# Linear attention with a mixture of experts on one core: the key sums of the last 24 head pairs, from TensorE's products with ones to a GpSimd reduction and a scatter

## The chip, the cores and the metric

The kernel runs on one core of a Trainium2 chip. The metric is the device time of one execution in microseconds, as the median of several runs. Lower is better.

## The reference, cut to what matters

Eight batches with eight heads each, 576 positions, head dimension 64, 128 features. Heads are taken in pairs: pair p holds two heads, and four pairs make a batch, so there are 32 pairs.

```
phi(x): proj = x @ w_phi; proj -= max|proj|;  [exp(proj), exp(-proj)]     # 256 features
kv  = sum over s of phi(k)[s,f] * v[s,d]        # 256 x 64 a head
z   = sum over s of phi(k)[s,f]                 # 256 a head
out = (phi(q) @ kv) / (phi(q) @ z + 1e-6)       # attention
x = out; four experts: causal softmax attention of x, times wo, weighted by the best two gates
```

The change is about z, the sum of phi(k) over the positions. phi(k) lies with positions on the partitions, so z is a sum over partitions.

## The kernel before, in words

All work is issued in an order that is written out: the strings `ORDER` and `SIDES` say, step by step, which of the kernel's streams (generators) goes on next and whether a copy goes to ScalarE or VectorE. Each engine carries out its instructions in exactly that order (`in_order` pins it), so an instruction that waits holds up all that stands behind it on its engine. The costs in `plan.run` and `plan.transfer` are a planner's bookings, used when the order was searched; they do not reach the chip.

Work for pair p of the 32:

- `stream_k`, `center`, `phi_k`: keys times w_phi on TensorE, centered on VectorE, exponentials on ScalarE. Four tiles of 128 positions for both heads end in `ek`; the last 64 positions of two pairs share one tile `ekt` (`stream_tails`).
- `key_sum` (pairs 4 to 31): the four position tiles are folded into one, [128, 512], called `zs`. ScalarE writes tiles 0 and 1 into zs; a GpSimd DMA adds tiles 2 and 3 on top (L373, zs<-ek); VectorE adds the two halves (L632); a second GpSimd DMA adds the tail (L373, zs<-ekt). What is left is a sum over 128 partitions. The first 4 pairs have no folding: TensorE sums all four tiles with ones.
- `stream_kv`: 32 matmul records of values times phi(k) (L692, tile shape 128x32), then z as products of `zs` with a matrix of ones (L704, four matmuls that show as eight records of 128 columns), all into one bank of PSUM with three parts a block, 384 columns. From pair 6 on (`KVD`), VectorE transposes the 384 columns out of PSUM into `kvt` (L723), four DMAs on the SP queue scatter it to a buffer in DRAM (kvd<-kvt), and one DMA brings it back as weights, kv (kv<-kvd). `kvd` and `kv` have two buffers.
- `stream_n`: denominators (L790, with the z columns of kv as weights) and numerators (L801) from phi(q) and kv. phi(q) needs a maximum over partitions for each head, which GpSimd forms (L763, PARTITION_ALL_REDUCE of 576 columns); VectorE subtracts it (L765).
- `stream_s`, `maxima`, `stream_t`: the experts' projections (L336), scores (L921), masks on GpSimd (L1029), softmax maxima on GpSimd (L1046, PARTITION_ALL_REDUCE of 1152 columns), attention (L1088, L1117) and the output projection (L336).

`in_order` also makes each PARTITION_ALL_REDUCE wait for the last VectorE instruction before it that takes two inputs from SBUF.

Of the kernel before, what the change touches and what calls it, by code (L numbers as in the profile page):

```python
# [53 lines left out]
KVD = 6  # L54
RATE = 2.18
# [26 lines left out]
def change_cost(a, b):  # L82
# [6 lines left out]
    r'2221111110333388AA27AB1EDE3AB68GC77F8FFG0000BC05BBBB2774@EGI@H@FBB@C@@C3;;1605B2;FFFEEF;FAA;77H6AA@B<JEIEC@C@6'  # L89
    r'BAGG830<8;58G;8II4;BHA;@B;E@<<818AB30F8C@B2;25B7CDC8:A7GCD6CE?EF38:C:BBBFGF;;;BBB00BFE1E24@GGF:5B3D?DE@D:@7FIG'  # L90
    r'72J:EBFD;;?IE:D?;6F6CD7CJCC79908I::432EGG?CD?IEIJGHDD@DEE;;:HH7IAIGG50:H7KG@G@IB?DDDDADDD61AFEB@F=:==:=H=IGA?:'
    r'32F9;9IE??99580EHGG6G6FFE<9E9F9F>>:::E@BFCBABCB963B<CDDB7GGFBDD<FFG7HDDE<HHA9<IHHG@85G8HGG:;=LIH?;;;;;;:HIHHCC'
    r'GGGIBFBHEEGFHGFB=@CAB:C>DA>6=6A48802888838501B?8;FFFAFDCCA=>BB@@:G::@999@?BED??HCDD?7HD8888@8CD78838CD@BGCF8:6'
    r'=FGBJDIJIC:IGH<>=5AGGFD:KGGE<CA9D98888@9D07F7CCHGG=?IIF<CG@HEE?@=828D@C<<DB99=985GGFB=D8FF76KED7JJI?EA?D?::D::'
    r'I:D:D:D<46123<HDCDDDC??=8888?88GE<E?<>CCF=D;839LE;F8<JICH8J988H888I:K5HH:DNGG8HM:J6JLGLJJJDA@BGB:MB:LLL:DJLD=B'
    r'HB::::<;AJKDD?GDAA>HHDEDEDA9IFAC66ACEEAA;;<B8CF7I8?=H?D057242:3K>@CC1E@@KBK>LB=<>LAJE@<<AAB>>ACFED<@IF<@E>?ECD'
    r'FG=B>H:I?CFE:HE:;HI<FGGGDG>?AA9989>88@J==8C008==IFKIFHJB<CEA>D<?@E@D8@>E9G@=>99G88>3CFFGFF>BBF77GGHG7J7III@KF8'
    r'5226GHIF99?18848J80?JNNIAJMJL88HHHHKJHHH>>;;;@876JJ>5B>K8L88>H>J7@D:::><NEFDH<IE::::FM>8G3C6HC88BBD2I?D89KICCJ'
    r'BIIBFBFFFE99FGBB?FF8843?E8888:FEF7I7J2HH@BFH:CJI6JJI:IA5@IA>KH@@H::GDB0A=;L>HHIH966;J?F<<MDHHIG:GMJJGGG?MEH:GK'
    r'KGE<<:<I@=GC?DC<CCCC?AMFCC<<:KB9LBJD>I;98883A8H=CB:B9A8EB=@E?F?F??:5ADEHGA<@CAAAFEFE<:HH7HH:HH7IIH08818880:J2J'  # L100
    r'JJC8CCDBCBBBB99F@D?GD@H83D98GGC?@G@H?7@H6F8G88888EHB5IF7ML<=B>>>Q<GH=D@DEDDDBHDID<A???G8<9KK9LLHD?<>;;;N985IG8'
    r'@<GMLOL0NM2884=M0377NGFIDMLJ?66DCDHHI:::C::::JLCKFM?88188FI<FC<KJ9K9LKEL=HC=FCG8888423888B:HFBG7JIDC?:II6IIII7'
    r'II>:5ONONIHEE:MF:::::1<HJJ8AJ>KIACAFBA;;;<IDJKKIHHNIFFADDIF69:==6=885DE?HE?BHC:K8BIBHBHCCGFEGEFFECBBA<JBHBBC<L'
    r'F300<K=<<99L9JL88<LI888883JKH8H:IIK8>BBBAI@7BG7GB:GH6JJL5NJGJHFJ:FJF9Q9R8<98K880=L4>2>881@8LGGGDD6IDDDDAGECG>E'
    r'8>=H=H==EI57N7EOGG>AAAAE@AFC?C999M>G6G882208838@KG>AIIDJJ>DAHIGHCCCGC99==IFF<G@EF::::JJ=I::BEBDC<KB<C?JHHHG?AJ'
    r'8BB8E:8==88F88848D7G67FHH>J><FFE<DDE5II7L=7;PMINIK>EHH@I;:IJ:ND:IJKJ:@3LACCCL6:K:KMKD6@:::L:;JFFG<JDEBEAEH@BGA'
    r'DDAGAFFADAD9E;CFF;GG88:II;F8:F?:LCCID5CC:HGFMHQKP<<<<GJFCH<F<BEBHHHAECNJCCHHK?KBMHBEAKK999PPCHH1N888308<2IA02H'
    r'I8CC8<>?8?8HFF@77D8=JKIIB4D5C6LI<KDKEEE?DJ>H>K<FC3EFB6<BA<<>9>GGG<@BB?DBA98988?888853E0EFE@EE877L><FGFFD<E>H?G'
    r'6F@AE2C998082@889GGH<FG>EE>C;;;FDGE8@EF<<GAD9IIIA9:=::J::LL:J:EE<HBGGGB?18?C77H=HHCCE:JJJ?G>>838C:KJ6J8KJJ:HII'
    r'GA@>F66A@5EFE:GJG@EE>FD::G:H:I::@9?F@?C?CCBBEBEDE??>D4888=1=71777C@<<@7<:::A96AB9A>=ADGFAFE0BC>>>49=62I9KCAMMA'  # L110
# [197 lines left out]
def tile_linear_attn_moe(ctx, tc, qt, kt, v, wts, out):  # L308
# [12 lines left out]
    def has(*k):  # L321
        return lambda: k in done
# [53 lines left out]
    warm = sb("warm", [128, 128], BF16)  # L376
    nc.vector.memset(warm, 1.0)
    col, ge = sb("col", [128, 128]), sb("ge", [128, 5, 4, 4])
# [30 lines left out]
    kvt = sb("kvt", [128, 4, 96])  # L409
# [26 lines left out]
    gw = col  # L436
# [187 lines left out]
    def key_sum(p, ek, ekk):  # L624
# [13 lines left out]
        done.add(('zt', p))  # L638
        done.add(('zs', p))
# [9 lines left out]
    def tail_products(banks, sums, m):  # L649
        ekt, need = ekts[m % 2], [f'et{m % 2}0', f'et{m % 2}1'] + vtk  # L650
        for h in range(2):
            for k in range(2):
                for a, (pk, ps) in enumerate(banks):
                    r = slice(64 * a, 64 * a + 64)
                    g = 64 * k + 32 * (h ^ a)
                    plan.run('PE', 256 / TRATE / 2 + 5, [pk], need, 64, tiling=(64, 32))
                    nc.tensor.matmul(three(ps)[g:g + 32, 0:2], vt_in[r, h, k:64:2], ekt[r, :, h].rearrange("p c (w f) -> p c w f", w=4),  # L657
                                     start=True, stop=False, skip_group_check=True)
# [8 lines left out]
    def three(ps):  # L667
        return ps[:, 0:384].rearrange("p (w c f) -> p c w f", w=4, c=3)

    def stream_kv():  # L670
# [3 lines left out]
        for p in range(NPAIRS):  # L674
# [10 lines left out]
            o = three(ps)  # L685
# [10 lines left out]
            if adds:  # L696
                yield Step('PE', pred=has('zs', p))
            for t in range(1 if adds else 4):
# [21 lines left out]
            else:  # L720

                yield Step('DVE', pred=has('kvs', p - 1) if p else None)
                dve(384, ['kvt'], [kc], 1.13).transpose(kvt.rearrange("p w n -> p (w n)"), ps[:, 0:384])  # L723
                plan.release('c', (kc, ps))

                for x in range(4):
                    yield Step('SP', pred=has('num', p - 2) if p > 1 else None)
                    load(kvd[p % 2].rearrange("w i x n -> i w x n")[:, :, x, :], kvt[32 * x:32 * x + 32], ('kvd', p % 2, x), ['kvt'])
                kd = [('kvd', p % 2, x) for x in range(4)]
                yield Step('SP')  # L730
# [515 lines left out]
```

## Time and profile before

| what | value |
|---|---|
| median of 3 runs | 575.58 us (574.83 to 576.74) |
| profiled execution: its time / its span | 575.26 us / 573.5 us |
| TensorE's granted clock in the profile | 1.00, that is its 2.4 GHz level, in all slices |
| TensorE (PE), VectorE (DVE), ScalarE (ACT), GpSimd (POOL) busy | 99%, 93%, 79%, 50% of the span |
| the chain that ended last, by engine | PE 92%, ACT 3%, all others 1% or less each |

The span is the stretch in which instructions of the program ran; the 1.8 us between it and the time lie around it. The chain follows the last instruction back, at each step to whatever released it. Busy time on PE is a union of modelled spans, so 99% says that matmuls followed on one another without holes, not that the array ran at its peak.

### The profile page before, as it was taken

How to read it: one execution, taken by the hardware profiler on the slowest of the kernel's cores; microseconds unless marked ns; L12 is line 12 of the kernel's file. 1: busy time of each engine (PE TensorE's matmuls, PEld its weight loads, DVE VectorE, ACT ScalarE, POOL GpSimd, SP SyncE). 2: the span in 40 equal slices, each digit the busy share in tenths (PEclk: the TensorE clock that was granted, in tenths of full speed). 3: DMA queues.
4: the chain of work that ended last, by engine and by line, in shares of the span. 5: the costliest groups of instructions: out<-in, count | busy, mean ns of one | idle time of the engine just before them, and what ended most of it. 6: DMA issues, size and time to landing. Idle time of an engine off the chain costs nothing.

```text
span 573.5 us, 19278 instructions
## 1 busy us (share of the span) xinstructions
PE 567.3 (99%) x7709; PEld 446.5 (78%) x7709; DVE 530.8 (93%) x1134; ACT 455.7 (79%) x1117; POOL 286.0 (50%) x223
## 2 busy tenths in 40 slices
PE   8999999999999999999999999999999999999997
PEld 6666697678877788768877878877887788789886
DVE  6998999999999999999999999999899999999983
ACT  5999989888888868988978887878877886756563
POOL 5467473655367255364735566334645457240530
PEclk9999999999999999999999999999999999999999
DMA  4779666563353653665565643567455462011013
GB/s 137 194 185 227 115 137 144 137 140 90 92 142 95 171 144 75 163 147 121 117 171 128 170 114 52 139 152 184 107 124 135 108 145 57 19 54 64 1 43 126
DMA packets 55785, 69.75 MB, mean 122 GB/s; under 512 B 29328, under 2 KB 34064, under 8 KB 55696
## 3 DMA queue, kind: packets, MB, share of 16 engines
q1 hardware_dynamic: 49184, 49.94, 29.8%
q0 software_dynamic: 6272, 18.35, 19.8%
q8 instruction: 61, 1.00, 0.8%
q10 hardware_dynamic: 240, 0.23, 0.1%
q14 instruction: 28, 0.23, 0.1%
HBM read 35.59 MB, written 14.55 MB: 87 GB/s over the span
## 4 chain that ended last, share of the span: by engine, by line
PE 92%; ACT 3%; DVE 1%; DMA 1%; SPq 1%; POOL 1%; issue 1%; DVEq 0%; POOLq 0%
PE ps_c L336 36%; PE ps_c L551 12%; PE ps_c L801 11%; PE ps_c L692 9%; PE ps_c L921 7%; PE ps_c L1117 7%; PE ps_c L790 5%; PE ps_c L1088 2%; PE ps_c L704 2%; PE ps_c L657 1%; SPq L369 1%; ACT ek L347 1%; DMA kvd<-kvt 1%; POOL mx L763 0%; PE ps_c L715 0%
## 5 line engine op out<-in xcount | busy, mean ns | idle before, releaser
L763 POOL PARTITION_ALL_REDUCE mx<-u x64 | 140.0, 2223 | 64.6 <-ACT u L345 33.7
L336 PE MATMUL ps_c<-x,qk 128*128 128x256 f32 (+1 forms) x768 | 106.9, 298 | 0.0
L336 PEld LDWEIGHTS ps_c<-x,qk 128*128 128x128 f32 x768 | 102.6, 189 | 2.7 <-ACT x L345 0.5
L1046 POOL PARTITION_ALL_REDUCE max<-top x16 | 57.6, 3598 | 42.1 <-DVE top L1042 19.8
L347 ACT ACTIVATE ek<-ek 128x1024 f32<-128x1024 f32 x64 | 67.9, 1061 | 8.3 <-DVE ek L619 7.7
L1029 POOL TENSOR_SCALAR_AFFINE_SELECT s<-s 128x256 f32<-128x256 f32 (+1 forms) x80 | 47.4, 636 | 49.1 <-ACT s L345 23.1
L345 ACT COPY s<-ps_c 64x64 f32<-64x64 f32 (+4 forms) x142 | 52.7, 430 | 15.1 <-PE ps_c L921 14.8
L1050 DVE TENSOR_TENSOR s<-s,max 128x1152 f32<-128x1152 f32 (+4 forms) x80 | 64.2, 835 | 0.4 <-POOL max L1046 0.3
L692 PE MATMUL ps_c<-ek,v_in 128*32 128x256 f32 x1024 | 61.5, 380 | 0.9 <-ACT u L345 0.9
L347 ACT ACTIVATE s<-s 128x384 f32<-128x384 f32 (+4 forms) x80 | 57.5, 739 | 2.9 <-DVE s L1050 2.7
L345 ACT COPY u<-ps_c 128x320 f32<-128x320 f32 (+1 forms) x126 | 46.4, 405 | 15.4 <-PE ps_c L551 12.5
L336 PE MATMUL ps_c<-yh,wo 128*128 128x320 f32 (+1 forms) x256 | 52.6, 300 | 0.0
L373 POOL DMA_DIRECT2D zs<-ek x28 | 25.6, 914 | 53.8 <-ACT ek L347 22.5
L692 PEld LDWEIGHTS ps_c<-ek,v_in 128*32 128x32 f32 x1024 | 32.5, 110 | 24.0 <-issue 3.3
L373 POOL DMA_DIRECT2D zs<-ekt x28 | 23.7, 845 | 55.2 <-DVE zs L632 28.8
L765 DVE TENSOR_TENSOR u<-u,mx 128x576 f32<-128x576 f32 x64 | 50.2, 795 | 0.7 <-POOL mx L763 0.7
L336 PE MATMUL ps_c<-vg,x 128*128 128x260 f32 x384 | 48.7, 285 | 0.4 <-ACT s L345 0.4
L336 PEld LDWEIGHTS ps_c<-vg,x 128*128 128x128 f32 x384 | 47.0, 188 | 1.3 <-ACT s L345 0.6
L1117 PE MATMUL ps_c<-s,vs 128*32 128x320 f32 (+4 forms) x896 | 47.2, 357 | 0.0
L616 DVE TENSOR_REDUCE pmax<-ps_c 128x4 f32<-128x512 f32 x64 | 42.4, 676 | 2.8 <-PE ps_c L551 2.6
L347 ACT ACTIVATE mx<-u 128x576 f32<-128x576 f32 x64 | 43.2, 686 | 2.0 <-DVE u L765 1.7
L1117 PEld LDWEIGHTS ps_c<-s,vs 128*32 128x32 f32 x896 | 29.4, 110 | 19.4 <-issue 0.6
(133 smaller groups left out, 1373.0 us busy)
## 6 DMA issues: line engine op xcount, KB each, us to landing
zs<-ek POOLq DMA_DIRECT2D x28, 512.0 KB, 5.2
q_in<-in_qt_dram SPq DMA_DIRECT2D x62, 144.0 KB, 3.2
k_in<-in_kt_dram SPq DMA_DIRECT2D x64, 128.0 KB, 3.3
v_in<-in_v_dram SPq DMA_DIRECT2D x32, 256.0 KB, 3.1
out_dram<-ot SPq DMA_DIRECT2D x28, 288.0 KB, 3.1
kvd<-kvt SPq DMA_DIRECT2D x104, 48.0 KB, 2.2
kv<-kvd SPq DMA_DIRECT2D x26, 192.0 KB, 2.5
zs<-ekt POOLq DMA_DIRECT2D x28, 128.0 KB, 3.4
```

Source lines behind the costliest of these rows:

```text
L336: nc.tensor.matmul(o, a, b, start=start, stop=stop, skip_group_check=True)
L345: nc.scalar.copy(o, i)
L347: nc.scalar.activation(o, i, func, **kw)
L373: nc.gpsimd.dma_start(o, i, accum_op=ALU.add)
L551: nc.tensor.matmul(o, a, b, start=True, stop=True, skip_group_check=True)
L692: nc.tensor.matmul(o[g, 0:2], v_in[:, 4 * h + t, k:64:2], ek[:, t, :, h, :].rearrange("p c (w f) -> p c w f", w=4), start=False, stop=t == ...
L763: nc.gpsimd.partition_all_reduce(M, U, 128, bass_isa.ReduceOp.absmax)
L765: dve(S, [uk], [mk], port=True).tensor_tensor(out=U, in0=U, in1=M, op=ALU.subtract)
L801: nc.tensor.matmul(ps[g:g + 32, 0:n], kvi[:, 2 * k + (h ^ p % 2), 32 * c:32 * c + 32], P_[h][c][:, s0:s1], start=c == 0, stop=c == 1, skip ...
L1046: nc.gpsimd.partition_all_reduce(big.rearrange("p e s -> p (e s)"), top.rearrange("p e s -> p (e s)"), 128, bass_isa.ReduceOp.max)
L1050: dve(2 * (S - 128 * j), [('d', x, j)], [('max', z)], 1.11, True).tensor_tensor(out=block(s_, j, None, rows(j)), in0=block(s_, j, None, ro ...
L1117: nc.tensor.matmul(ps[r:r + 32, q0 - s0:s1 - s0], vs[:, j, 128 * g + 64 * e + k:128 * g + 64 * e + 64:2], ss[x][:, e, o + q0:o + s1], star ...
```

## The change

`ZP = 8`: pairs 0 to 7 stay as they are. For pairs 8 to 31:

1. The products of zs with ones (L704) are gone. PSUM holds two parts, 256 columns, instead of three, and TensorE's kv products no longer wait for zs.
2. A PARTITION_ALL_REDUCE with add on GpSimd sums zs over the partitions into `zr` [128, 512], after the tail's add.
3. One DMA on the SP queue scatters row 0 of zr to kvd, column 64: 512 runs of one 4-byte word, beside the four DMAs of kv.
4. VectorE's transpose out of PSUM takes 256 columns, and the four DMAs carry 64 columns a block in place of 96. The load of kv waits for five transfers, not four.
5. `warm`, `kvt`, `zr` and `col` become parts of one tile, `shared`; kvt and zr overlap where only pairs before 8 use kvt, and the gates' weights get a tile of their own.
6. `ORDER` (3143 steps in place of 3119) and `SIDES` (520 in both) are new throughout.

```diff
+ZP = 8
 ORDER = (
...
-    kvt = sb("kvt", [128, 4, 96])
+    shared = sb("shared", [128, 768])
+    kvt, zr = shared[:, 0:384].rearrange("p (w n) -> p w n", w=4), shared[:, 256:768]
...
         done.add(('zt', p))
+        if p >= ZP:
+            zk = ['zr', 'kvt'] if p == ZP else ['zr']
+            yield Step('POOL', pred=lambda: p != ZP or ('kvs', p - 1) in done)
+            plan.run('POOL', 3235, zk, k, port=2100)
+            nc.gpsimd.partition_all_reduce(zr, o, 128, bass_isa.ReduceOp.add)
+            yield Step('SP', pred=has('kvs', p - 2))
+            plan.transfer(900, 560, [('kvd', p % 2, 'z')], ['zr'], 'SP')
+            nc.sync.dma_start(kvd[p % 2][:, :, :, 64:65].rearrange("w i x n -> n x (w i)"), zr[0:1, :].rearrange("o (x f) -> o x f", x=4))
         done.add(('zs', p))
...
-            o = three(ps)
+            o = three(ps, 3 if p < ZP else 2)
...
-            if adds:
+            if adds and p < ZP:
                 yield Step('PE', pred=has('zs', p))
-            for t in range(1 if adds else 4):
+            for t in range(0 if p >= ZP else 1 if adds else 4):
...
-                dve(384, ['kvt'], [kc], 1.13).transpose(kvt.rearrange("p w n -> p (w n)"), ps[:, 0:384])
+                n = 384 if p < ZP else 256
+                src = shared[:, 0:n]
+                dve(n, ['kvt'], [kc], 1.13).transpose(src, ps[:, 0:n])
...
-                kd = [('kvd', p % 2, x) for x in range(4)]
-                yield Step('SP')
+                kd = [('kvd', p % 2, x) for x in (range(4) if p < ZP else (0, 1, 2, 3, 'z'))]
+                yield Step('SP', pred=has('zs', p) if p >= ZP else None)
                 load(kv[p % 2].rearrange("p x n -> p (x n)"), kvd[p % 2].rearrange("w i x n -> (w i) (x n)"), f'kv{p % 2}', kd)
```

## Rows read from the trace of the kernel before

**Rows 1.** The page's part 1: busy us, share of the span, instructions.
```profile
PE 567.3 (99%) x7709; PEld 446.5 (78%) x7709; DVE 530.8 (93%) x1134; ACT 455.7 (79%) x1117; POOL 286.0 (50%) x223
```

**Rows 2.** All waits of PE: waiter <- who ended it, us, times, longest.
```profile
PE ps_c L336 <- DVE col L380: 1.0, 1, 1.0
PE ps_c L692 <- ACT u L345: 0.9, 1, 0.9
PE ps_c L336 <- ACT s L345: 0.4, 1, 0.4
PE ps_c L801 <- DVE wided L812: 0.2, 1, 0.2
```

**Rows 3.** Busy us of each engine, 95 to 490 us: pairs 8 to 31.
```profile
95.00:490.00 395.00, 394.31 (x5414) 307.18 (x5408) 375.92 (x796) 323.38 (x803) 210.16 (x165) 1.00 0.54 126
```

**Rows 4.** The chain, 95 to 490 us, by line.
```profile
by line: PE ps_c L336 35.5%; PE ps_c L551 11.4%; PE ps_c L801 11.0%; PE ps_c L692 9.9%; PE ps_c L921 7.2%; PE ps_c L1117 6.7%; PE ps_c L790 5.5%; PE ps_c L657 1.7%; PE ps_c L1088 1.5%; PE ps_c L704 1.2%; SPq L369 1.1%; DMA kvd<-kvt 0.8%; is
```

**Rows 5.** PE by line, 95 to 490 us: busy us, mean ns, idle before.
```profile
L704 PE MATMUL ps_c<-zs,ones 128*32 128x128 f32 x192 | 9.8, 273 | 0.0
```

**Rows 6.** PE in order of time at 286 us: start, us, line.
```profile
286.21 0.40 PE L704 MATMUL ps_c<-zs,ones 128*32 128x128 f32 x8
286.54 1.16 PE L551 MATMUL ps_c<-wf,k_in 64*128 64x128 f32 x16
```

**Rows 7.** The chain, 297 to 312 us: start, us, what, count.
```profile
300.93 0.22 PE ps_c L704 x8
...
309.93 0.22 PE ps_c L704 x8
```

**Rows 8.** DVE by line, 95 to 490 us, same columns as rows 5.
```profile
L765 DVE TENSOR_TENSOR u<-u,mx 128x576 f32<-128x576 f32 x46 | 37.2, 815 | 0.3 <-POOL mx L763 0.3
...
L632 DVE TENSOR_TENSOR zs<-zs 128x512 f32<-128x512 f32 x23 | 18.4, 800 | 0.0
...
L723 DVE STREAM_TRANSPOSE kvt<-ps_c 128x384 f32<-128x384 f32 x24 | 13.7, 569 | 2.6 <-PE ps_c L704 1.4 <-DMA kvd<-kvt 1.0
...
L812 DVE STREAM_TRANSPOSE wided<-ps_c 128x288 f32<-128x288 f32 x23 | 10.7, 464 | 0.5 <-PE ps_c L790 0.5
```

**Rows 9.** POOL by line, 95 to 490 us, same columns as rows 5.
```profile
L763 POOL PARTITION_ALL_REDUCE mx<-u x46 | 101.0, 2231 | 42.8 <-ACT u L345 19.8 <-DVE s L1050 10.4 <-ACT x L345 4.9
L1046 POOL PARTITION_ALL_REDUCE max<-top x12 | 43.1, 3590 | 31.0 <-DVE top L1042 17.9 <-DVE u L765 4.8 <-DVE facy L824 4.4
```

**Rows 10.** DMA issues: queue, count, KB each, median us to landing.
```profile
kvd<-kvt SPq DMA_DIRECT2D x104, 48.0 KB, 2.2
kv<-kvd SPq DMA_DIRECT2D x26, 192.0 KB, 2.5
zs<-ekt POOLq DMA_DIRECT2D x28, 128.0 KB, 3.4
```

**Rows 11.** Lines L765 and L632, whole span: ns minimum/median/maximum.
```profile
L765 DVE TENSOR_TENSOR u<-u,mx x64: 692/748/2124, 10.6 to 489.7; 128x576 f32<-128x576 f32 x64
...
L632 DVE TENSOR_TENSOR zs<-zs x28: 627/679/1898, 44.6 to 476.3; 128x512 f32<-128x512 f32 x28
```

**Rows 12.** All DMAs on kvd: us to landing; the SP queue's wait on them.
```profile
DMA to landing us min/median/max: 1.5/2.4/6.3
...
SPq L369 <- DMA kvd<-kvt: 33.6, 24, 3.7
```

**Rows 13.** The SP queue at 303 us, in order of time: start, us, count.
```profile
302.87 1.75 SPq L369 DMA_DIRECT2D kvd<-kvt  x4
```

**Rows 14.** Load of kv and its first product, pairs 28 and 20, in order of time.
```profile
452.19 0.34 SPq L369 DMA_DIRECT2D kv<-kvd  x1
457.62 0.69 PE L790 MATMUL ps_c<-mx,kv 128*32 128x288 f32 x8
...
310.51 0.53 SPq L369 DMA_DIRECT2D kv<-kvd  x1
317.48 0.67 PE L790 MATMUL ps_c<-mx,kv 128*32 128x288 f32 x8
```

More of the change, by code (lines that the diff above doesn't have):

```diff
@@ L94 @@
[L94 to L98, printed above, removed]
@@ new lines @@
+    r'4<1HH=H996I9A9II49127BD<FCB<<<B33==BADHGD99C;461EDDEFG@@;8B8IEIJ:3B:D1ED;DDG;C<<<;HH745A@CCF@AGHF8IFH@6GG;GFH8'
+    r';K7G@7;F0HDEEFBBDDDC;;;77HJIH@AGFHH:EDGGHH9;J;KHIJJFFII2188:23:5JJ00:@47L6L7JJF@??FCCEEE@====EECB:9<?@CCG989CD'
+    r'>B:95EEG>>3D9D6>>6DEFEE19<B9FEEEBEAC@9CC:::DDEEBF@EF96<BCE7HGFE<FFEEE78:;IH8C8C;H5IJIIDEFF;;;;;;KHGGA3>6?HEE=I'
+    r'@EEEEEE808881848;HF80HA@BDCC?;=@A503A>D;8@6=:JJEBGG=:??@FFF=ABAB?CA@@=?@@::?:999282888?D?GG?HH?EFCDAEA88483B@:'
+    r'CDC7D7FE5>>C:H@H<<68@H?ADJ999KCBLFCHCG888GCI=77<H8JGI?B2>==H8BG8G0E8FDE9AA97CH<JAD5GHI7L<>=888283=81G0EGEJ=69G'
@@ L126 @@
+    r'00000000000000000100011011000000100000000000000000000000001000000000100000000000000010110000100000001000000000'
+    r'00000000000000000000110010000000000001000001000000100100000000000000010000000010000000010001010000000100001100'
+    r'00000000001001000000001100010010100000100100100000000011010000110001010001001110'
 )
@@ L373, in add_to @@
         nc.gpsimd.dma_start(o, i, accum_op=ALU.add)
-    warm = sb("warm", [128, 128], BF16)
+    shared = sb("shared", [128, 768])
+    kvt, zr = shared[:, 0:384].rearrange("p (w n) -> p w n", w=4), shared[:, 256:768]
+    warm = shared[:, 640:704].bitcast(BF16)
     nc.vector.memset(warm, 1.0)
-    col, ge = sb("col", [128, 128]), sb("ge", [128, 5, 4, 4])
+    col, ge = shared[:, 512:640], sb("ge", [128, 5, 4, 4])
     row = ge.rearrange("p t a b -> p (t a b)")[:, 0:32]
@@ L656, in tail_products @@
                     plan.run('PE', 256 / TRATE / 2 + 5, [pk], need, 64, tiling=(64, 32))
-                    nc.tensor.matmul(three(ps)[g:g + 32, 0:2], vt_in[r, h, k:64:2], ekt[r, :, h].rearrange("p c (w f) -> p c w f", w=4),
+                    nc.tensor.matmul(three(ps, n)[g:g + 32, 0:2], vt_in[r, h, k:64:2], ekt[r, :, h].rearrange("p c (w f) -> p c w f", w=4),
                                      start=True, stop=False, skip_group_check=True)
@@ L665, in tail_products, with three @@
                     nc.tensor.matmul(three(ps)[g:g + 32, 2], ones[r, :], ekt[r, c, h].rearrange("p (w f) -> p w f", w=4), start=False, stop=False, skip_group_check=True)
-    def three(ps):
-        return ps[:, 0:384].rearrange("p (w c f) -> p c w f", w=4, c=3)
+    def three(ps, c=3):
+        return ps[:, 0:128 * c].rearrange("p (w c f) -> p c w f", w=4, c=c)
     def stream_kv():
@@ L727, in stream_kv @@
                     yield Step('SP', pred=has('num', p - 2) if p > 1 else None)
-                    load(kvd[p % 2].rearrange("w i x n -> i w x n")[:, :, x, :], kvt[32 * x:32 * x + 32], ('kvd', p % 2, x), ['kvt'])
-                kd = [('kvd', p % 2, x) for x in range(4)]
-                yield Step('SP')
+                    load(kvd[p % 2].rearrange("w i x n -> i w x n")[:, :, x, 0:n], src[32 * x:32 * x + 32], ('kvd', p % 2, x), ['kvt'])
+                kd = [('kvd', p % 2, x) for x in (range(4) if p < ZP else (0, 1, 2, 3, 'z'))]
+                yield Step('SP', pred=has('zs', p) if p >= ZP else None)
                 load(kv[p % 2].rearrange("p x n -> p (x n)"), kvd[p % 2].rearrange("w i x n -> (w i) (x n)"), f'kv{p % 2}', kd)
```

61 lines of the change are left out of this document (30 added, 31 removed).

## The prediction, as it was put on record before the run

> **What bounds the kernel now.** I read the shares of the page first: TensorE is busy 99% of the span, VectorE 93%, GpSimd 50% [rows 1]. A busy TensorE alone proves little, so the waits come next. All of its waits together are 2.5 us, in four places, and none of them is on the key sums, on kv or on GpSimd [rows 2]. Then the stretch that the change touches: the products with ones of pairs 8 to 31 lie between 95 and 490 us. In these 395 us TensorE is busy 394.3, VectorE 375.9 and GpSimd 210.2 [rows 3], and the chain goes through TensorE line after line [rows 4]. So here the time is TensorE's work, and VectorE has 19.1 us of room (395 - 375.9), 4.8%: the next bound stands close behind. GpSimd has 185 us of room. Work taken from TensorE comes off the time as long as VectorE, GpSimd and the transfers can follow a schedule that is a little denser.
>
> **The change part by part.**
>
> *Products with ones, removed from TensorE.* Per pair eight records go, 192 for 24 pairs [rows 5]. Three views give three prices. The union of their spans is 9.8 us [rows 5], which is too much, since each span of 273 ns overlaps the next ones. From the start of the group to the start of what follows it is 286.54 - 286.21 = 0.33 us [rows 6]; that holds the emptying of the array before another tile shape (128x32 to 64x128). That step isn't saved: the products L692 ahead of the group have the same shape, and the change of shape then falls after them. The chain, which counts from the end of L692's last product to the end of the group's last, gives 0.22 us for each of the two groups shown [rows 7]. 24 x 0.22 = 5.3 us. The share of the chain agrees: 1.2% of 395 us is 4.7 us [rows 4]. I take 5.3, with 4.7 and 24 x 0.33 = 7.9 as ends. No copy of this work remains on TensorE.
>
> *VectorE's transpose, 384 to 256 columns.* 569 ns for 384 columns, 464 for 288 [rows 8], so 105 ns per 96 columns; 128 fewer save 140 ns, 24 x 0.14 = 3.4 us of VectorE. Off the path, but it is room for the next item.
>
> *The reduction on GpSimd, added.* The trace has the same instruction with another operator: 2.23 us for 576 columns, 3.59 for 1152 [rows 9]. For 512 columns the line through both gives 2.1 us; an add might cost as much as the larger one, 3.6. The plan's booking in the diff, 3.235, lies between, and its bookings for the two known ones (2.125, 3.49) are within 5% of the rows, so I take 3.2. 24 x 3.2 = 77 us, ends 50 and 86. GpSimd goes from 210 to 287 of some 390 us, 74%: it fits, and hides in its idle time. What it costs if that cover is gone: the reduction must wait for the tail's add to land, 3.4 us after its issue [rows 10]. Queued behind it on GpSimd are the masks (L1029), the maxima of phi(q) (L763), for which VectorE's L765 waits, and the next pair's adds. If it always stood at the head of the queue for the whole 3.4 us, 24 x 3.4 = 82 us more would bring GpSimd to 369 of 390 us. The new order has to put other GpSimd work in between, and the 185 us of room allow it.
>
> *Its hold on VectorE.* VectorE instructions with two inputs from SBUF are at times stretched: L765 has a median of 748 ns and a maximum of 2124, L632 679 and 1898 [rows 11], about one reduction's length longer. The means in the stretch are 815 and 800 [rows 8], so the excess over the medians is 46 x 0.067 + 23 x 0.121 = 5.9 us, for 46 + 12 = 58 reductions [rows 9]: 0.10 us each. 24 more cost 2.4 us at that rate; below at 0, and at most 24 x 1.38 = 33 us if each one catches an instruction for 2124 - 748 ns. I take 2.4, since the new reductions wait for VectorE's last two-input instruction just like the old ones. With the 3.4 us saved, VectorE stands at 375.9 - 3.4 + 2.4 = 374.9 of 395 - 5.3 = 389.7 us: room of 14.8 us in place of 19.1. For that I let TensorE's few waits grow in proportion to the reductions in the stretch, 82 to 58: 2.5 us [rows 2] times 0.4 = 1.0 us. Ends: 0 and 3.
>
> *The scatter of z and the chain to kv.* Nothing in the trace has runs of one word. The nearest rows are the DMAs to the same buffer: median 2.2 us to landing for kvd<-kvt, 128 runs each [rows 10], 1.5 at the least [rows 12]. Below, the scatter lands in the same 2.2; above, four times as many runs take four times the part over 1.5, so 1.5 + 4 x 0.7 = 4.3. I take 3.0. The old chain after the tail's add: group 0.33, transpose 0.57, three of the four issues, at 1.75 / 4 = 0.44 each [rows 13], ahead of the last one's landing, 2.2: about 4.4 us. The new one: reduction 3.2, an issue ahead of the landing, up to 0.6, landing 3.0: 6.8, so 2.4 us later, ends 0.4 and 4.1 (2.1 and 2.2; 3.6 and 4.3). kv's own transfers now run beside it. What covers the 2.4 us: from the issue of kv's load to the first product on it the nine tightest of the 24 pairs have 5.4 us (pair 28) to 7.0 (pair 20), the other fifteen more [rows 14]. The load takes 2.5 [rows 10], so the shortest rooms are 2.9 to 4.5 us, and 2.4 fits into each. Cost: nothing. The SP queue already stands 33.6 us in 24 waits for kvd [rows 12]; the loads of keys, queries and values behind it stand as before or a little longer, and no wait of TensorE ends at them now [rows 2].
>
> On the width of the scatter the Trainium skill has a rule that speaks against the change (DMA: Bandwidth & Descriptors, section "Why a DMA increments its semaphore by 16 and not by 1"): a transfer uses as many engines, up to 16, as divide the slowest dimension on both sides. Here that is 4, so four engines would have 128 words each to write where kvd<-kvt gives each of sixteen 8 runs; no run here shows this. By it the scatter would be an estimate of 16 times 0.7 us over 1.5, some 13 us, and the kv rival below would come to pass.
>
> The Trainium skill also has a price for a sum over partitions (GPSIMD Engine Reference, section 3.2): 247,699 ns for 128x2048 with a tensor_reduce. By it 24 sums of 512 columns would be an estimate of 1.5 ms; [rows 9] have 2.2 us for 576 columns with the instruction used here, so the trace doesn't agree and decides.
>
> *Order and shared tile.* The new order moves everything. That costs nothing as such; a few changes of tile shape more or less, at 0.33 - 0.22 = 0.11 us each, are inside my ends. The shared tile saves space and adds waits only around pair 8: nothing.
>
> *Sum.* 575.26 - 5.3 + 1.0 = 571.0 us for an execution like the profiled one. That one lies 0.3 us below the median of the runs, so the forecast for a median is 571.3. Its own range: 575.6 - 7.9 = 567.7 up to 575.6 - 4.7 + 3 = 573.9.
>
> **The rivals.**
>
> *VectorE becomes the bound.* For it: only 4.8% of room [rows 3], and 24 more reductions on the resource that stretches L765 and L632 [rows 11]. Against it: 0.10 us a reduction so far [rows 8, 9]. It takes over when the reductions cost more than 14.8 + 2.4 = 17 us, 0.7 us each, which is every second one catching an instruction for 1.38 us; at 0.93 each (22.5 us) the whole gain is gone: 575.6. Its time: 574 to 577.
>
> *kv comes late (slower).* Place: the wait of L790 for kv's load, behind the scatter. Price: nine pairs have a room of 2.9 to 4.5 us, mean about 3.8; at x us later than now they lose 9 (x - 3.8). It turns the sign from x = 4.4 on (9 x 0.6 = 5.4). That needs a scatter of some 5 us, just over my upper end, in place of 3. With x = 5: 575.6 - 5.3 + 10.8 = 581; with x = 6: 590. For it: nothing in the trace has such small runs. Against: only 512 words, and an order that was searched with a booking for this transfer could widen the rooms.
>
> *More than forecast.* The change of shape is saved too and kv's bank is free earlier: 567.4 or less.
>
> *It does not do what it says.* That the products stay can be excluded from the diff: the loop over them is empty from pair 8 on.
>
> **How the numbers follow.** A measurement of this kernel can tell some 0.3%, 1.7 us, from no change, so faster is below 573.9 and slower above 577.3. Forecast 0.70 (567.7 to 573.9), more 0.05, VectorE as the bound 0.15 (574 to 577), kv late 0.10 (578 to 590). The range 568 to 576 takes in the forecast and two thirds of the VectorE case, 0.8 in all. Faster 0.70 + 0.05 = 0.75; same 0.15; slower 0.10.
>
> **What would show each step.** Right: 32 records of L704 on zs in place of 224, the 24 groups of 0.22 us gone from the chain, TensorE's waits in the low single microseconds, 24 new reductions of 2 to 3.6 us, L723 near 430 ns for 256 columns, L765 and L632 with means within 50 ns of now. Wrong: waits of TensorE at L790 or L801 ended by kv's load, or a scatter that lands after more than 5 us (kv late); VectorE above 97% in the stretch with many stretched L765 and L632 (VectorE's bound); GpSimd standing long at the new reduction while L765 waits for L763.

## The result: the changed kernel is slower

The changed kernel takes 581.99 us (581.01 to 584.62), the kernel before 576.73 us (574.83 to 576.88) on the same chip. The ratio on record is 1.0105, 95% interval 1.0080 to 1.0131: by it 6 us slower (5.3 us between the medians), where 4.3 us faster was forecast. The profiled execution took 581.99 us, its span is 580.2 us.

The page's part 1 of the changed kernel (busy us, share of the span, instructions), against [rows 1]:

```profile
PE 568.6 (98%) x7517; PEld 441.7 (76%) x7517; DVE 532.4 (92%) x1134; ACT 459.8 (79%) x1117; POOL 368.9 (64%) x247
```

The 192 products are gone from TensorE, and yet it is not busy for less time: 568.6 us. GpSimd has its 24 reductions more. The stretch of pairs 8 to 31 again, against [rows 3] (us; then busy us and count of PE, PEld, DVE, ACT, POOL; granted clock, DMA share, GB/s):

```profile
95.00:490.00 395.00, 389.50 (x5150) 298.20 (x5150) 369.20 (x781) 324.55 (x798) 281.72 (x183) 1.00 0.55 122
```

TensorE now stands idle for 5.5 us of the stretch (395 - 389.50), where it stood 0.7. VectorE has become less busy (375.9 to 369.2, the shorter transposes and the slower pace), so it is not the bound. TensorE's granted clock is full speed in both. All the larger waits of TensorE (waiter <- who ended it: us, times, longest), against [rows 2]:

```profile
PE ps_c L703 <- DMA v_in<-in_v_dram: 1.5, 3, 0.6
PE ps_c L804 <- DMA kv<-kvd: 1.2, 2, 1.0
PE ps_c L935 <- DVE shared L736: 1.1, 1, 1.1
PE ps_c L337 <- DVE shared L383: 1.1, 1, 1.1
PE ps_c L553 <- DMA k_in<-in_kt_dram: 1.0, 1, 1.0
```

All waits together are 7.8 us, where they were 2.5, and 4.0 us of them now end with a transfer, where none did: values (v_in), keys (k_in and kt_in), and kv itself. 1.4 us of these 4.0 lie before 23 us, ahead of the first reduction (99.6 us), so at most 2.6 us can come from the new work. The chain that ended last is TensorE for 73% of the span, where it was 92%. That is a sign, not yet the cause: the reductions, the scatter and the new order came in one change. (The lines have moved: L704 of before is L715, L790 L804, L801 L815, L763 L777, L765 L779, L723 L736, L632 L634; the reduction is L645, the scatter L648.)

### The profile page after: what moved, and what is told of

Read it like the earlier page. It is cut to its first block, busy times and chain, and to the rows that moved or that the text cites. A ratio compares the mean times of both kernels' runs of the same rounds, so it can differ in the third digit from the quotient of the medians.

```text
span 580.2 us, 18980 instructions
## 1 busy us (share of the span) xinstructions
PE 568.6 (98%) x7517; PEld 441.7 (76%) x7517; DVE 532.4 (92%) x1134; ACT 459.8 (79%) x1117; POOL 368.9 (64%) x247
## 3 DMA queue, kind: packets, MB, share of 16 engines
q1 hardware_dynamic: 61568, 48.42, 30.2%
## 4 chain that ended last, share of the span: by engine, by line
PE 73%; DVE 10%; DMA 5%; ACT 5%; SPq 4%; issue 2%; POOL 1%; DVEq 0%; POOLq 0%; ACTq 0%
PE ps_c L337 29%; PE ps_c L553 9%; PE ps_c L815 9%; PE ps_c L703 8%; PE ps_c L935 5%; PE ps_c L1131 5%; SPq L370 4%; PE ps_c L804 4%; DMA v_in<-in_v_dram 2%; DVE top L1056 2%; DMA kvd<-shared 1%; PE ps_c L668 1%; PE ps_c L1102 1%; DVE u L779 1%; DMA kv<-kvd 1%
## 5 line engine op out<-in xcount | busy, mean ns | idle before, releaser
L777 POOL PARTITION_ALL_REDUCE mx<-u x64 | 142.8, 2255 | 48.3 <-DVE u L779 14.6
L645 POOL PARTITION_ALL_REDUCE shared<-zs x24 | 79.6, 3315 | 6.8 <-DVE u L779 4.4
L1043 POOL TENSOR_SCALAR_AFFINE_SELECT s<-s 128x256 f32<-128x256 f32 (+1 forms) x80 | 50.7, 672 | 31.6 <-ACT s L346 30.6
L1064 DVE TENSOR_TENSOR s<-s,max 128x1152 f32<-128x1152 f32 (+4 forms) x80 | 68.6, 898 | 0.6 <-POOL max L1060 0.5
L346 ACT COPY s<-ps_c 128x448 f32<-128x448 f32 (+4 forms) x148 | 55.1, 428 | 17.2 <-PE ps_c L935 15.4
L348 ACT ACTIVATE s<-s 128x1152 f32<-128x1152 f32 (+4 forms) x80 | 57.3, 741 | 4.6 <-DVE s L1064 4.4
L346 ACT COPY u<-ps_c 128x256 f32<-128x256 f32 (+1 forms) x115 | 43.2, 403 | 20.2 <-PE ps_c L553 15.5
L779 DVE TENSOR_TENSOR u<-u,mx 128x576 f32<-128x576 f32 x64 | 52.9, 835 | 0.0
L553 PE MATMUL ps_c<-q_in,wf 64*128 64x256 f32 (+1 forms) x256 | 47.9, 437 | 0.9 <-DVE x L341 0.4
```

Source lines behind the costliest of these rows:

```text
L346: nc.scalar.copy(o, i)
L348: nc.scalar.activation(o, i, func, **kw)
L553: nc.tensor.matmul(o, a, b, start=True, stop=True, skip_group_check=True)
L645: nc.gpsimd.partition_all_reduce(zr, o, 128, bass_isa.ReduceOp.add)
L777: nc.gpsimd.partition_all_reduce(M, U, 128, bass_isa.ReduceOp.absmax)
L779: dve(S, [uk], [mk], port=True).tensor_tensor(out=U, in0=U, in1=M, op=ALU.subtract)
```

## Experiments

The theory that they had to test was the prediction's: GpSimd's idle time hides the reductions, kv's room hides the scatter, and the order is free. The rivals were three: the reductions cost time (through GpSimd's queue, or through their hold on VectorE), the scatter costs time (through kv's wait, or through the transfers beside it), and the new order costs time by itself. Kernels called old_ have the order of the kernel before, those called new_ the changed one. Times are medians with their lowest and highest; ratios are to the kernel before, run on the same chip beside them, with 95% intervals (they differ by up to 0.2% from the ratio of the two medians). Differences are taken between ratios, and 0.1% is 0.58 us. Line numbers shift by a few from kernel to kernel.

Not all expectations held. new_no_sum came out between what the theories wanted; new_no_reduce (580.15 us), new_by_x (586.39) and new_nowait (593.56) lie above every value expected of them.

### The order alone, and what the products were worth

*old_no_sum*: the old order without products, reductions and scatters; transposes and kv's transfers in their shorter form. The edit is shown against the changed kernel; `ORDER` and `SIDES` are those of the kernel before.

```diff
-            if adds and p < ZP:
+            if adds:
                 yield Step('PE', pred=has('zs', p))
...
-            nc.gpsimd.partition_all_reduce(zr, o, 128, bass_isa.ReduceOp.add)
...
-            nc.sync.dma_start(kvd[p % 2][:, :, :, 64:65].rearrange("w i x n -> n x (w i)"), zr[0:1, :].rearrange("o (x f) -> o x f", x=4))
...
-                yield Step('SP', pred=has('zs', p) if p >= ZP else None)
+                yield Step('SP')
```

> The order of the kernel before, without the products with ones of pairs 8 to 31 and with the shorter transposes and kv transfers, and nothing in their place. Left out: z of pairs 8 to 31. It measures the first term of the prediction by itself: 0.22 us a pair, so 5.3 us below the kernel before, 571.4 us. If the time follows the 0.33 us from start to start instead: 568.8. If TensorE was not the bound there: 575 to 577.

*new_no_sum*: the changed kernel, the new order kept, without reductions and scatters.

```diff
-            nc.gpsimd.partition_all_reduce(zr, o, 128, bass_isa.ReduceOp.add)
...
-            nc.sync.dma_start(kvd[p % 2][:, :, :, 64:65].rearrange("w i x n -> n x (w i)"), zr[0:1, :].rearrange("o (x f) -> o x f", x=4))
```

> The changed kernel with its new order, but without the 24 reductions on GpSimd and without the 24 scatters; the load of kv waits for the four kv transfers alone. Left out: z of pairs 8 to 31 (old words stay in the buffer). Theory S (the scatter, its wait on the SP queue and kv behind it make the loss): about 571 us, 11 below the changed kernel's 582. Theory V (24 more reductions hold VectorE): also about 571. Theory O (the new order itself is the worse one, with 181 changes of tile shape for 167 and more waits): 578 to 580.

Measured: old_no_sum 570.70 us (569.91 to 573.31), ratio 0.9912 (0.9881 to 0.9943); new_no_sum 574.92 us (574.63 to 577.49), ratio 0.9986 (0.9970 to 1.0002). The two issue the same work and differ only in `ORDER` and `SIDES`, that is in its order and in which copies go to ScalarE or VectorE, and their times don't overlap. Part 1 of their pages, old_no_sum first:

```profile
PE 562.9 (99%) x7517; PEld 440.9 (77%) x7517; DVE 527.1 (93%) x1134; ACT 456.1 (80%) x1117; POOL 286.2 (50%) x223
```

```profile
PE 565.9 (99%) x7517; PEld 440.1 (77%) x7517; DVE 526.5 (92%) x1134; ACT 459.5 (80%) x1117; POOL 291.4 (51%) x223
```

Two things follow. The products, with the shorter transposes and transfers that go with them, were worth 0.88%, 5.1 us, so the first term of the sum holds. And the new order (with its `SIDES`) costs 0.74%, 4.3 us, before anything is done in it. Its waits are nearly the same, 3.3 us against 3.0; with the same 7517 instructions TensorE is busy 3.0 us longer. Counted over TensorE's records, the tile shape changes 179 times in new_no_sum (181 in the changed kernel) and 167 times in old_no_sum and in the kernel before. Twelve more at the prediction's 0.11 us are 1.3 us. The Trainium skill gives a reason for such a price (TensorEngine Tiling (Array Packing), section Key Properties: a change of the tiling mode drains TensorE); the 0.33 us against 0.22 of [rows 6, 7] fit it. No line shows the other 3 us: they stay open.

### The reductions alone

*new_no_scatter* (and *new_no_scatter2*, the same kernel beside other runs): the new order with the reductions, without the scatters.

```diff
-            nc.sync.dma_start(kvd[p % 2][:, :, :, 64:65].rearrange("w i x n -> n x (w i)"), zr[0:1, :].rearrange("o (x f) -> o x f", x=4))
```

> The changed kernel with its reductions, but without the scatters and without the load's wait for them. Left out: z of pairs 8 to 31 does not reach kv. S: about 572 us, nearly all of the loss gone. V: 579 to 582, nearly nothing gone. O: 579 to 582.

> new_no_scatter once more, in more rounds, as the partner of new_fill2: 580.1 us as before. Left out: z of pairs 8 to 31 does not reach kv. The difference to new_fill2 is the price of the reductions' hold on VectorE; theory V wants 4 to 5 us, theory Q 0 to 2.

*new_fill* (and *new_fill2*): as new_no_scatter, but in place of the reduction GpSimd does work of the same length that reads almost nothing: one column copied (so that it waits for the same sum) and six memsets of 128x512.

```diff
-            nc.gpsimd.partition_all_reduce(zr, o, 128, bass_isa.ReduceOp.add)
+            nc.gpsimd.tensor_copy(zr[:, 0:1], o[:, 0:1])
+            for _ in range(6):
+                nc.gpsimd.memset(zr, 0.0)
```

> The changed kernel in its new order without scatters, as new_no_scatter (580.1 us), but each reduction is replaced by a copy of one column (which waits for the same transfers) and six memsets of 128x512 on GpSimd, about as long together (near 3 us) and without reading SBUF. Left out: z of pairs 8 to 31. It splits the 5.2 us between new_no_sum (574.9) and new_no_scatter (580.1). Theory V (the reduction's reading holds VectorE's two-input instructions): 575 to 576. Theory Q (GpSimd's queue is occupied, masks and maxima behind it come late, whatever occupies it): 579 to 581.

> new_fill once more, in more rounds beside new_no_scatter2: it had 578.4 us with runs from 577.2 to 581.8. Left out: z of pairs 8 to 31. If occupying GpSimd costs most of the reductions' 5.2 us: 578 to 579.5. If the reading of SBUF costs most: 575 to 576.5.

*new_nowait*: as new_no_scatter, but the 24 reductions don't wait for VectorE's last instruction with two inputs from SBUF.

```diff
-        elif pairs is not None and type(i).__name__ == 'InstPartitionAllReduce':
+        elif pairs is not None and type(i).__name__ == 'InstPartitionAllReduce' and not any(x.bass_ap.tensor.name.startswith('shared') for x in i.outs if hasattr(x, 'bass_ap')):
```

> new_no_scatter (580.1 us), but the 24 added reductions do not wait for VectorE's last two-input instruction; the other 80 still do. Left out: z of pairs 8 to 31 does not reach kv. If that wait, with the masks and maxima queued behind it, is what costs: 576 to 578. If the wait protects VectorE and GpSimd from each other: 580 to 583. If neither: 580.

Measured: new_no_scatter 580.11 us (579.70 to 581.90), ratio 1.0074 (1.0049 to 1.0098), and 580.54, 1.0072 (1.0050 to 1.0094) as new_no_scatter2. new_fill 578.38 us (577.22 to 581.79), 1.0056 (1.0032 to 1.0080), and 578.72, 1.0049 (1.0025 to 1.0072), as new_fill2. new_nowait 593.56 us (591.36 to 595.28), 1.0303 (1.0269 to 1.0336).

Over new_no_sum the reductions cost 0.88 and 0.86%, 5.1 us; the filling costs 0.70 and 0.63%, some 3.8 us. So by these numbers about three quarters of the price is that GpSimd is taken for 3.3 us at these places, whatever it does there. The share is rough. Three of the seven runs of each filling had a mean granted clock of 0.994 to 0.997 and took 1 to 5 us more than the others; in the profile of new_fill2 the clock is 0.89 between 15 and 30 us, where TensorE waits 2.4 us for values, ahead of the first filling, and 1.00 afterwards. By the medians of the runs at 0.999 or more the filling costs 0.49 and 0.65%, the reductions 0.85 and 0.81%: 60 to 80%. The rest, 0.2 to 0.4%, is not told from nothing by these times, and two things are in it: the reductions read SBUF, and they wait for VectorE's last two-input instruction, which the filling does not. That the reductions cost VectorE time the busy rows show: L779 (L765 of before) by line on VectorE, 95 to 490 us, in new_no_sum, new_fill and new_no_scatter (count | busy us, mean ns | idle before):

```profile
L777 DVE TENSOR_TENSOR u<-u,mx 128x576 f32<-128x576 f32 x45 | 33.4, 746 | 0.0
```

```profile
L780 DVE TENSOR_TENSOR u<-u,mx 128x576 f32<-128x576 f32 x46 | 35.5, 776 | 0.0
```

```profile
L778 DVE TENSOR_TENSOR u<-u,mx 128x576 f32<-128x576 f32 x46 | 39.2, 856 | 0.0
```

The reductions stretch it from 746 to 856 ns, the filling to 776. What the reductions would do without their wait new_nowait shows: 2.3% more than new_no_scatter, 13 us. TensorE's mean granted clock is lower there too, 0.991 to 0.997 in the four runs; how much of the 13 us that is was not measured apart. The wait is worth keeping. The Trainium skill (SBUF — State Buffer, section "Who interferes with whom") says that GpSimd's port pair is VectorE's second one and that only this pair causes contention, as an exclusive lock; by that rule a two-input instruction can stand for as long as a reduction has the pair. The trace of the changed kernel agrees: its longest L779 took 3021 ns and started 0.14 us after a reduction, whose lengths are 3226 to 3837 (rows below).

In which queue the 3.8 us are paid is not seen in one wait. From new_no_sum to new_no_scatter TensorE's waits go from 3.3 to 6.9 us: those on VectorE's results from 1.7 to 4.1, those on transfers from 1.6 to 2.8. The waits on transfers all lie before 24 us, ahead of the first reduction, so only those on VectorE can be its work. VectorE in its turn waits for GpSimd for 1.4 us only. So the delay reaches TensorE through a row of small steps, and that it starts at masks and maxima that come late is argued, not shown.

### The old order has no place for them

*old_no_scatter*: the reductions in the old order, where the products stood. *old_change*: the scatters too, behind the last of kv's four transfers.

```diff
             if p >= ZP:
                 for _ in range(4):
                     plan.run('PE', 55, [kc], [f'z{zp}'], tiling=(128, 32))
+                nc.gpsimd.partition_all_reduce(zr, zs[:, zp].rearrange("p c h f -> p (c h f)"), 128, bass_isa.ReduceOp.add)
```

> old_change (619.1 us) without its scatters: the reductions stand in the old order where the products stood. Left out: z of pairs 8 to 31 does not reach kv. The 48 us over old_no_sum (570.7) are split. If the reductions cost through GpSimd's queue and VectorE, in an order that has no gap for them: 605 to 619. If kv's load behind the scatter makes them: 575 to 580.

> The whole change in the old order: each reduction stands on GpSimd where the products stood on TensorE, each scatter on the SP queue right behind the fourth kv transfer. Nothing is left out. O: 572 to 574 us, a gain on the kernel before. S: 580 or more, as kv comes later than in the old order, whose tightest nine pairs have 2.9 to 4.5 us of room. V: 576 to 580.

Measured: old_no_scatter 617.01 us (616.23 to 617.54), ratio 1.0687 (1.0663 to 1.0711); old_change 619.09 us (618.05 to 621.62), 1.0749 (1.0711 to 1.0787). GpSimd by line in old_no_scatter, 95 to 490 us (count | busy us, mean ns | idle before it <- who ended it):

```profile
L773 POOL PARTITION_ALL_REDUCE mx<-u x42 | 93.2, 2251 | 22.2 <-DVE gw L1012 8.0 <-DMA zs<-ek 4.6 <-ACT vs L346 4.2
L704 POOL PARTITION_ALL_REDUCE shared<-zs x21 | 69.9, 3329 | 34.0 <-DVE max L1072 12.0 <-DVE s L1060 9.2 <-DVE u L775 6.0
```

In front of 21 reductions GpSimd stands 34.0 us, 27.2 of them for three of VectorE's two-input instructions, with masks and maxima queued behind it; in the changed kernel it stands 6.8 us in front of 23 (below). The queue is served in order, and at the old places the reductions cost 44.6 us (1.0687 - 0.9912 = 7.75%) and not nothing. The chain that ended last goes through TensorE for 42% of the span, VectorE for 32% and GpSimd for 11%, where TensorE has 90% in old_no_sum. A part of the 44.6 us is TensorE's clock: its mean is 0.98 between 95 and 490 us, with falls to the 1.2 GHz level at 146, 221, 307 and 413 us, where waits of 1.2 to 4.8 us lie. An estimate from these two numbers is 395 x 0.02, some 8 us. The scatters on top cost 0.62% (1.0749 - 1.0687; the intervals touch), so the 580 or more that theory S wanted came for another reason than the scatter. The new order thus does what it is for: it takes 44.6 us down to 5.1. But it pays 4.3 us for it.

### The scatter alone

*new_no_reduce*: the new order without reductions; a constant row is scattered to an unused column, and kv's load waits for that.

```diff
-            nc.gpsimd.partition_all_reduce(zr, o, 128, bass_isa.ReduceOp.add)
...
-            nc.sync.dma_start(kvd[p % 2][:, :, :, 64:65].rearrange("w i x n -> n x (w i)"), zr[0:1, :].rearrange("o (x f) -> o x f", x=4))
+            nc.sync.dma_start(kvd[p % 2][:, :, :, 65:66].rearrange("w i x n -> n x (w i)"), zr[0:1, :].rearrange("o (x f) -> o x f", x=4))
```

> The changed kernel without the 24 reductions, with the 24 scatters and the load's wait for them; they write a constant to an unused column (65), from a row set once at the start. Left out: z of pairs 8 to 31. Beside new_no_sum (574.9 us) it prices the scatter when it never waits for GpSimd. If the scatter's 4 us before kv's load are what it costs: 576 to 577, as much as the 1.9 us between new_no_scatter and the changed kernel. If its cost is the SP queue's wait for GpSimd, with the loads behind it: 575.

*new_scatter_free*: the same words to a buffer of their own; nobody waits. *new_row_only*: the same bytes to such a buffer, written as 16 runs of 128 B in place of 512 words. On the chip it became a single run: its trace has one packet of 2048 bytes and one of 4 for each of these transfers. *old_scatter_free*: the free scatter in the old order.

```diff
+    zd = [dp.tile([4, 32, 4, 96], F32, name=f"zd{i}") for i in range(2)]
...
+            nc.sync.dma_start(zd[p % 2][:, :, :, 0:1].rearrange("w i x n -> n x (w i)"), zr[0:1, :].rearrange("o (x f) -> o x f", x=4))
```

```diff
+    zd = [dp.tile([1, 16, 32], F32, name=f"zd{i}") for i in range(2)]
...
+            nc.sync.dma_start(zd[p % 2], zr[0:1, :].rearrange("o (a f) -> o a f", a=16))
```

> As new_no_reduce (580.15 us: scatters, no reductions), but the 512 words go to a buffer of their own in DRAM, so that kv's load does not wait for them; their issue on the SP queue, their words and their rings stay the same. Left out: z of pairs 8 to 31. If kv's load behind the scatter is what costs 5.2 us (products with kv late, loads behind on the SP queue late): 575 to 576, the time of new_no_sum (574.9). If the words' traffic or the issues cost it: 579 to 580.

> As new_scatter_free (580.06 us), but the same 2 KB go to their own buffer in 16 runs of 128 bytes instead of 512 runs of one word. Issue and place on the SP queue stay. Left out: z of pairs 8 to 31. If the words on the rings hold up the loads issued behind them: 575 to 576, like new_no_sum (574.9). If the additional issue on the SP queue costs by itself: 579 to 580.

> The old order as in old_no_sum (570.7 us), with 24 scatters of 512 words of a constant row to a buffer of their own, on the SP queue behind the fourth kv transfer; no load waits for them. Left out: z of pairs 8 to 31. If the words cost about 5 us wherever they stand: 575 to 576. If it is the new order alone that has no room for them on the SP queue: 571 to 572.

| kernel | median us (lowest to highest) | ratio (95% interval) |
|---|---|---|
| new_no_sum, for comparison | 574.92 (574.63 to 577.49) | 0.9986 (0.9970 to 1.0002) |
| new_row_only | 576.97 (575.59 to 579.05) | 1.0006 (0.9985 to 1.0027) |
| new_scatter_free | 580.06 (578.09 to 582.24) | 1.0062 (1.0036 to 1.0088) |
| new_no_reduce | 580.15 (578.57 to 581.06) | 1.0068 (1.0042 to 1.0093) |
| old_scatter_free | 575.00 (571.98 to 577.20) | 0.9955 (0.9934 to 0.9975) |

The scatter with its wait costs 0.82%, 4.7 us (1.0068 - 0.9986). Without anybody waiting it costs 0.76%, so kv's wait is worth no more than the 0.06% between, which is nothing that these intervals show. As one run in place of 512 words it costs 0.20%, within the intervals nothing: so it is not that there is one more transfer, but the 512 words, 0.56%, 3.2 us. (Five of the ten runs of new_row_only have a mean granted clock of 0.996 or 0.997; in its profile it is 0.89 between 15 and 30 us, where TensorE waits 2.2 us for values, ahead of the first transfer of a row. By the runs at 0.999 or more the row costs nothing and the words 0.7%.) In the old order the free scatter costs 0.43%, 2.5 us (0.9955 - 0.9912; the intervals just overlap).

Where the words cost shows on the SP queue. The same piece of it around one transfer of z (start us, us, count), new_scatter_free first, then new_row_only:

```profile
305.87 0.66 SPq L650 DMA_DIRECT2D zd<-shared  x1
306.58 2.37 SPq L370 DMA_DIRECT2D kvd<-shared  x2
308.99 2.39 SPq L370 DMA_DIRECT2D k_in<-in_kt_dram  x2
```

```profile
306.95 0.29 SPq L650 DMA_DIRECT2D zd<-shared  x1
307.28 0.78 SPq L370 DMA_DIRECT2D kvd<-shared  x2
308.11 1.11 SPq L370 DMA_DIRECT2D k_in<-in_kt_dram  x2
```

The issue itself takes 0.66 us for words and mostly 0.29 for the row. The issue right behind it takes 1.5 to 2.6 us in the 16 of 24 places where one follows at once, against 0.3 to 1.1 in the same places of new_row_only. So the words hold up the issues behind them in the queue. What in the queue or the rings does it, no run shows. Of TensorE's waits between 95 and 490 us two are in new_scatter_free, at 251 and 314 us, and not in new_row_only or new_no_sum; new_no_reduce has the same two:

```profile
PE ps_c L806 <- ACT zs L348: 1.2, 1, 1.2
PE ps_c L556 <- DMA k_in<-in_kt_dram: 1.0, 1, 1.0
```

The second is a load of keys. The first is most likely the load of kv: L806 does not read the zs that the profile names, and the last step of that load's semaphore comes at 250.84 us, 0.14 us before the product starts. So kv's load does come late, but without waiting for the scatter: its own transfers are issued late behind it. These two waits are 2.2 us; the rest of the 3.2 us is not seen in one line.

### Two other ways to bring z to kv

*new_by_x*: the whole change, with the scatter cut into four transfers of 128 words.

```diff
-            nc.sync.dma_start(kvd[p % 2][:, :, :, 64:65].rearrange("w i x n -> n x (w i)"), zr[0:1, :].rearrange("o (x f) -> o x f", x=4))
+            [nc.sync.dma_start(kvd[p % 2][:, :, x, 64:65].rearrange("w i n -> n (w i)"), zr[0:1, 128 * x:128 * x + 128]) for x in range(4)]
```

> The whole change, nothing left out, with each scatter cut into four of 128 words, one for each of the four blocks of 128 features. In the changed kernel the 512 words run from 1.2 to 3.3 us after the issue, about 240 a microsecond. If the number of engines at work grows with the cut (more words a microsecond) and the landing counts: 581 us, up to 1 below the changed kernel. If three more issues on the SP queue weigh more: 583 to 584.

*new_two_hops*: the whole change, but z goes to a DRAM buffer as in new_row_only; kv's load of 64 columns doesn't wait for it, and a second load brings z's column, word by word.

```diff
+            nc.sync.dma_start(zd[p % 2], zr[0:1, :].rearrange("o (a f) -> o a f", a=16))
...
+                    nc.sync.dma_start(kv[p % 2][:, :, 0:64], kvd[p % 2].rearrange("w i x n -> (w i) x n")[:, :, 0:64])
+                    nc.sync.dma_start(kv[p % 2][:, :, 64:65], zd[p % 2].rearrange("o a f -> (o a f)").rearrange("(x f n) -> f x n", x=4, n=1))
```

> The whole change, nothing left out, with another way for z: row 0 of zr goes to DRAM in 16 runs of 128 bytes, kv's load takes 64 columns a block and waits for its own four transfers alone, and a second load right behind it brings z to its column, four words on each of 128 partitions. kv's load no longer waits for z. If the scatter's 4 us ahead of kv's load are the cost: 578 to 580, 2 to 4 below the changed kernel's 582. If the SP queue's standing for GpSimd and the number of its issues cost: 582 to 585.

Measured: new_by_x 586.39 us (583.12 to 589.28), ratio 1.0179 (1.0134 to 1.0224), 0.74% above the changed kernel: its 96 transfers land 2.1 us after their issue in the median, but the four issues take the SP queue 2.46 us in place of 0.66 (at 236 us and at 231 us). Since the issue behind the single scatter is slow as well, that alone does not explain the 0.74%, and the rest stays open. new_two_hops 580.01 us (578.97 to 581.67), ratio 1.0068 (1.0044 to 1.0092): 0.37%, 2.1 us, below the changed kernel, with intervals that overlap (1.0080 to 1.0092). It is still slower than the kernel before. No version that computes all of z was faster than the kernel before; the way of bringing z has at most the 5.1 us to win that lie between old_no_sum and it.

## Why the prediction was wrong, step by step

The account, each step from ratios: products -0.88%, order +0.74%, reductions and scatters together +1.19% (1.0105 - 0.9986; alone 0.88 and 0.82%, so a part of their delays is the same delay). That is +1.05%: -5.1 + 4.3 + 6.9 = 6.1 us. The prediction had -5.3 + 1.0.

*Products with ones, -5.3 us: right*, 5.1 measured. Of the three prices, the chain's step from end to end was the one to take.

*"Order and shared tile": the step that failed first.* It let the order cost nothing as such and left a few changes of shape inside the ends. The order costs 4.3 us. What it had not asked is what an order that makes room on one engine gives up on another: 12 more changes of shape (1.3 us by the prediction's own price), and 3 us that stay open.

*The reduction on GpSimd: size right, cover wrong.* The length was taken as 3.2 us. GpSimd by line, 95 to 490 us, and the reduction and L779 over the whole span (ns minimum/median/maximum, first and last start) in the changed kernel, against [rows 9, 11]:

```profile
L777 POOL PARTITION_ALL_REDUCE mx<-u x45 | 100.9, 2266 | 23.6 <-DVE u L779 5.7 <-DVE zs L634 4.9 <-DVE facy L838 4.0
L645 POOL PARTITION_ALL_REDUCE shared<-zs x23 | 76.2, 3315 | 6.8 <-DVE u L779 4.4 <-DVE max L1076 0.9 <-DVE s L1064 0.5
```

```profile
L645 POOL PARTITION_ALL_REDUCE shared<-zs x24: 3226/3253/3837, 99.6 to 499.2; - x24
...
L779 DVE TENSOR_TENSOR u<-u,mx x64: 682/746/3021, 11.8 to 505.5; 128x576 f32<-128x576 f32 x64
```

3253 ns, and GpSimd at 282 us in the stretch, near the 287 forecast. "It fits, and hides in its idle time" was wrong: at the old places 24 reductions cost 44.6 us, at the searched ones 5.1. The idle 185 us of [rows 3] were read as room, but they lie in pieces between masks and maxima for which others wait, in a queue that is served in order; that this is how the price comes about is argued, not shown. The prediction's own sign for this (GpSimd standing long at the reduction while L779 waits) does not show in the changed kernel, 6.8 us in all; it shows in old_no_scatter.

*Its hold on VectorE, 2.4 us of VectorE.* L779 and L634 have means of 850 and 682 ns in the changed kernel, 815 and 800 before: within the 50 ns for one, 118 ns less for the other. Against new_no_sum, the proper comparison, the reductions give L779 110 ns more. "About one reduction's length longer" was no fair reading of [rows 11]: 2124 - 748 is 1.38 us, a reduction 2.23. In the changed kernel it does hold, 3021 - 746 = 2.28 us. In the time the hold is at most the 0.2 to 0.4% left over by the filling, so of 1.0 us with ends 0 and 3 nothing is refuted. *VectorE as the bound* did not come: 93.5% (369.2 of 395) with 95.2% before.

*The transpose* has 441 ns for 256 columns, where 430 was expected; the time of the whole is not told apart by it.

*The scatter: landing near the upper end, "Cost: nothing" wrong.* The SP queue at 231 us in the changed kernel, scatter and kv's load behind it (start us, us), against [rows 13]:

```profile
231.31 0.66 SPq L648 DMA_DIRECT2D kvd<-shared  x1
...
235.34 0.35 SPq L370 DMA_DIRECT2D kv<-kvd  x1
```

The load goes 4.0 us after the scatter's issue (3.9 to 4.7 at the six other places where it stands right behind one); 3.0 was taken for the landing, 4.3 was the upper end. TensorE waits for kv's load twice, 0.22 us at 196 us and 0.98 at 253. The larger place, first on the SP queue with the scatter and kv's own four transfers, then in the chain (start us, us, what):

```profile
241.42 0.65 SPq L648 DMA_DIRECT2D kvd<-shared  x1
...
243.78 4.27 SPq L370 DMA_DIRECT2D kvd<-shared  x4
```

```profile
246.92 3.48 DMA kvd<-shared
...
250.53 2.53 DMA kv<-kvd
253.05 0.14 issue
253.19 1.18 PE ps_c L804 x16
```

The load's first product stands 2.7 us behind its issue, the tightest place; [rows 14] had 5.4 us. But what the load waits for here is not the scatter, issued 9.1 us before it: it is the last of kv's own four transfers, issued at 246.92. Behind the scatter the four take the queue 4.27 us, where [rows 13] has 1.75. So the rival of a late kv names a thing that happens, 1.2 us in two places, and its time (578 to 590) holds the result, but its mechanism, the load waiting for the scatter's landing, is not the cause: without anybody waiting the scatter costs the same. What the step left out are the scatter's neighbours in the queue. "No wait of TensorE ends at them now" was read as room for the loads, and the chain near 311 us shows one that has become late; its issue, too, stands shortly behind a scatter (308.08 us):

```profile
311.19 4.74 DMA k_in<-in_kt_dram
315.93 0.14 issue
316.06 0.46 PE ps_c L553 x2
```

In the list of DMA issues of before a load of keys lands after 3.3 us in the median; here it takes 4.74 us, and TensorE waits for it. Neither bound for the scatter held a term for what it does to the issues and transfers behind it.

*The number of engines.* Between some 1.2 and 3.3 us after the issue the trace has about 240 words a microsecond, 16.7 ns a word over four engines. The Trainium skill's rule that the prediction weighed (DMA: Bandwidth & Descriptors, section "Why a DMA increments its semaphore by 16 and not by 1"), four engines for this shape, fits that, as do the packets (516 for a scatter, four more than its words), though the trace does not name the engines; the estimate of 13 us that the prediction drew from it does not, since 128 words an engine take about 2 us.

*The chances.* Faster had 0.75 and slower 0.10, because each new cost was held against an idle resource by itself, and for the three of them (reduction, scatter, order) the answer was nothing or 1 us. They measured 5.1, 4.7 and 4.3 us, each by itself.

## What to carry to other kernels

Where one engine is busy 99% of the span and all the others are scheduled around it, as here, the idle time of another engine or queue is not yet a cover: what a place in the order costs is measured by putting an empty filling of the same length there before anything else is built. When a change brings a new order, run the new order with the new work left out, so that its own price is known; here it ate 4.3 of the 5.1 us to be won. Count a transfer by its runs and by what is issued behind it in its queue, not by its bytes and its own consumer. And look at when a wait lies before it is put down to a change: the waits for values before 24 us are there without the reductions and scatters, too.

## What was not expected of the hardware

- 24 transfers of 512 words, 2 KB each, cost 3.2 us more than 24 of the same bytes in one run, with nobody waiting for them; the issue right behind one took 1.5 to 2.6 us on SP. In the page's part 3 (packets, MB, share of the engines' time) the queue grows from 49184 to 61568 packets, 24 times 516, and its share only from 29.8 to 30.2%:

```profile
q1 hardware_dynamic: 61568, 48.42, 30.2%
```

- Reductions that don't wait for VectorE's two-input instructions are dear: 24 of them cost 13 us more than with the wait, some 0.6 us each.
- Mere memsets on GpSimd, 24 times 3.4 us with nothing that reads their result, cost 3 to 4 us in a kernel in which GpSimd is idle for a third of the span (busy 65%).
